# First feed-forward of a packed-attention kernel: block by block over both halves, output products of 512 tokens, a ninth tile for the rest

## The chip, the cores and the metric

The kernel runs on one core of one Trainium2 chip, as one launch with no arithmetic on the host. The metric is device time in microseconds (us) of that core, the median of several runs. The engines are PE (TensorE, matmuls; PEld is its weight load), DVE (VectorE), ACT (ScalarE), POOL (GpSimd) and SP (SyncE, which issues the DMAs).

## The reference, cut to what matters

```python
# q, k, v: (8, 8, 576, 64); p: (8, 8, 32, 64): 8 batches, 8 heads, 576 tokens, 32 packed rows
p_packed = softmax(scale * p @ k.T) @ v
out      = softmax(scale * q @ p_packed.T) @ p_packed
x = out.transpose(0, 2, 1, 3).reshape(4608, 512)
# first feed-forward, d_ff 1536
xn = x / sqrt(mean(x * x) + 1e-6) * rms_g
x1 = (silu(xn @ w_gate) * (xn @ w_val)) @ w_out
# second feed-forward, d_ff 2048
h = x1 @ w_in
return (h * cos(h)) @ w2_out
```

All weights come as 64-bit floats and are narrowed on the chip to 32 bits with integer operations; every large product is made of three matmuls over a high and a low part of both operands (`mm3`, L152 to L155).

## The kernel before, in words

**First stage.** The packed rows are computed for all batches and heads (L599 to L652). Beside it, weights are narrowed: `narrow_a` is an ACT operation and, for some weights, one of POOL; `narrow_b` is three or four operations of DVE (L139 to L148). A weight's `narrow_b` is put off to `w_late` (L640), which is called at the end of the round or, for the last rounds, at the top of the next (L625); those of the last two weights come at L625 of round 17. The attention of batch 0 (`bg0`) runs beside it from round 5; its last four steps come after the stage (L758).

**First feed-forward.** The loop at L811 has one round for each of 8 x 2 x 12 blocks: a batch `b`, a half `hf` of 288 tokens, a block `f` of 128 of the 1536 columns. In batches 1 to 7 the order is half 0 with all 12 blocks, then half 1. In batch 0 it is four blocks of half 0, the same four of half 1, and so on (`SEG`, L795), since its weights are still being narrowed. A round does this:
- `gv_block` (L696): 12 matmuls of 288 columns for gate and value, into two of the four PSUM tiles of the tag `mm`; then a sigmoid on ACT (L710) and two products on DVE (L711, L712), which read and so release those two tiles.
- `split_s` (L715): high part on ACT (L103), low part on DVE (L104), each of 288 tokens.
- `acc_block` for the block of two rounds before (`LAG`): 12 matmuls of 288 columns (four parts of 128 outputs, three each) into four PSUM tiles. When a half is complete (in batch 0: when four blocks of a half are), the sums are copied to `x1` by DVE (L743) and ACT (L744); in batch 0 the second and third groups of four are added to the first by DVE (L737). The result goes to DRAM (L746).
- `att_step`, twice in a round: steps of the attention of the batch after, a generator (`attend`, L215). It is given out evenly over the 48 slots of a batch (`N_ATT`, L802; in batch 0 from slot 10). Its PSUM tiles are `mm` too. Counts 13 and 14 are the two exponentials (L249), which need another ACT table than the sigmoid.
- at the rounds in `units`: `unit` (L540), which multiplies packed rows by narrowed weights (16 matmuls, `mps`, two `mm` tiles) and splits the result for a batch to come (ACT L103 and DVE L104, `wmhl`), followed by `wy_fetch`, the load of weights for the unit after the next.
- in batch 0, `b0_step` (L534): one weight of `B0_W` a round, `narrow_b` of the one before, the split of the one before that.
- from round 28, at seven rounds of a batch (`W2_AT`), one of the 32 tiles of the weights of the second feed-forward: load, `narrow` in one piece, store (L675 to L691).

**Second feed-forward.** Nine chunks of 512 tokens, 16 blocks each: `h_block` (12 matmuls of 512 columns), cosine on ACT and DVE (L888 to L894), product and split (`h_rest`), and `o_block`, three blocks later (`LAG_B`; 12 matmuls of 512 columns). The first chunk and the first weights are loaded and split in the last batch of the first feed-forward (L830 to L845, L857 to L861).

**Order.** Each engine works its instructions in the order of the program text as far as `order` reaches (L597 to block 6 of the second feed-forward, `OWN`); after that the framework's scheduler orders them. All DMAs are issued by SP, in order.

## Time and profile before

| | |
|---|---|
| runs | 1751.84, 1753.54, 1756.1 us; median 1753.54 us |
| profiled execution | 1755.67 us, of which its span is 1753.9 us |
| PE busy | 1676.0 us, 96% of the span |
| DVE busy | 1121.2 us, 64% |
| ACT busy | 835.9 us, 48% |
| POOL busy | 67.6 us, 4% |
| mean granted PE clock | 0.979 |

Matmuls overlap in the pipeline, so one of them is shown longer than the time by which it delays the next; what a stream of matmuls costs is the distance from one start to the next. PEclk is the granted clock as a share of 2.4 GHz; its lower level is 1.2 GHz. An idle time in brackets stands before the instruction, with what ended it. A wait is put down to the one that ended last.

### The profile page before, as it was taken

How to read it: one execution, taken by the hardware profiler on the slowest of the kernel's cores; microseconds unless marked ns; L12 is line 12 of the kernel's file. 1: busy time of each engine (PE TensorE's matmuls, PEld its weight loads, DVE VectorE, ACT ScalarE, POOL GpSimd, SP SyncE). 2: the span in 40 equal slices, each digit the busy share in tenths (PEclk: the TensorE clock that was granted, in tenths of full speed). 3: DMA queues.
4: the chain of work that ended last, by engine and by line, in shares of the span. 5: the costliest groups of instructions: out<-in, count | busy, mean ns of one | idle time of the engine just before them, and what ended most of it. 6: DMA issues, size and time to landing. Idle time of an engine off the chain costs nothing.

```text
span 1753.9 us, 28300 instructions
## 1 busy us (share of the span) xinstructions
PE 1676.0 (96%) x11184; PEld 1454.7 (83%) x11184; DVE 1121.2 (64%) x2184; ACT 835.9 (48%) x1599; POOL 67.6 (4%) x77
## 2 busy tenths in 40 slices
PE   7776879999999999999999999999999999999998
PEld 5555768999999999999999788888888888888887
DVE  2576887767767676766565765556565656555554
ACT  3454454444444444444445654555454545454443
POOL 0000331000000000000002000000000000000000
PEclk8887999999999999999999999999999999999999
DMA  9996543345353525332234200000000000000010
GB/s 205 254 270 187 145 128 121 130 147 173 133 179 102 193 96 185 129 119 76 87 104 154 73 24 25 24 25 24 25 24 25 24 25 24 25 1 25 0 25 24
DMA packets 88260, 164.89 MB, mean 94 GB/s; under 512 B 24128, under 2 KB 46656, under 8 KB 88128
## 3 DMA queue, kind: packets, MB, share of 16 engines
q1 hardware_dynamic: 88128, 163.09, 30.6%
q8 instruction: 88, 1.44, 0.3%
q14 instruction: 44, 0.36, 0.1%
HBM read 127.93 MB, written 35.13 MB: 93 GB/s over the span
## 4 chain that ended last, share of the span: by engine, by line
PE 81%; DVE 7%; DMA 6%; issue 4%; ACT 2%; SPq 1%; POOL 0%; DVEq 0%; ACTq 0%; POOLq 0%
PE ops L155 7%; PE ops L153 7%; PE ops L154 7%; PE hp L155 7%; PE hp L154 7%; PE hp L153 7%; PE gv L153 5%; PE acc L153 5%; DMA kn<-in_k_dram 5%; PE acc L154 5%; PE acc L155 5%; PE gv L154 5%; PE gv L155 5%; PE mps L548 3%; PE sp L233 1%
## 5 line engine op out<-in xcount | busy, mean ns | idle before, releaser
L153 PE MATMUL gv<-apt,wmhl 128*128 128x288 f32 x768 | 238.4, 310 | 12.1 <-DVE silu L711 9.3
L153 PE MATMUL acc<-shl,wohl 128*128 128x288 f32 x768 | 234.6, 305 | 1.0 <-ACT sq L293 1.0
L154 PE MATMUL acc<-shl,wohl 128*128 128x288 f32 x768 | 228.6, 298 | 0.0
L155 PE MATMUL acc<-shl,wohl 128*128 128x288 f32 x768 | 228.5, 297 | 0.0
L154 PE MATMUL gv<-apt,wmhl 128*128 128x288 f32 x768 | 228.0, 297 | 0.0
L155 PE MATMUL gv<-apt,wmhl 128*128 128x288 f32 x768 | 227.3, 296 | 0.0
L153 PE MATMUL ops<-w2hl,ghl 128*128 128x512 f32 x576 | 224.8, 390 | 1.7 <-ACT ghl L103 1.7
L154 PE MATMUL ops<-w2hl,ghl 128*128 128x512 f32 x576 | 224.8, 390 | 0.0
L154 PE MATMUL hp<-xhl,wmhl 128*128 128x512 f32 x576 | 224.1, 389 | 0.0
L155 PE MATMUL hp<-xhl,wmhl 128*128 128x512 f32 x576 | 224.1, 389 | 0.0
L153 PE MATMUL hp<-xhl,wmhl 128*128 128x512 f32 x576 | 224.1, 389 | 0.0
L155 PE MATMUL ops<-w2hl,ghl 128*128 128x512 f32 x576 | 223.2, 391 | 0.0
L901 DVE TENSOR_TENSOR r<-r,hp 128x512 f32<-128x512 f32 x144 | 98.9, 687 | 179.1 <-ACT r L894 179.0
L893 ACT ACTIVATE r<-r 128x512 f32<-128x512 f32 x144 | 91.1, 632 | 247.9 <-DVE r L892 247.9
L103 ACT ACTIVATE shl<-silu 128x288 fp32r<-128x288 f32 x192 | 85.3, 444 | 240.4 <-DVE silu L712 238.4
L153 PEld LDWEIGHTS gv<-apt,wmhl 128*128 128x128 f32 x768 | 145.3, 189 | 53.4 <-DVE silu L711 13.2
L888 ACT ACTIVATE kk<-hp,magic 128x512 f32<-128x512 f32 x144 | 99.1, 689 | 121.9 <-PE hp L155 121.9
L153 PEld LDWEIGHTS acc<-shl,wohl 128*128 128x128 f32 x768 | 145.6, 190 | 1.2 <-ACT sq L293 1.2
L154 PEld LDWEIGHTS gv<-apt,wmhl 128*128 128x128 f32 x768 | 145.9, 190 | 0.0
L154 PEld LDWEIGHTS acc<-shl,wohl 128*128 128x128 f32 x768 | 145.6, 190 | 0.0
L155 PEld LDWEIGHTS gv<-apt,wmhl 128*128 128x128 f32 x768 | 145.5, 189 | 0.0
L155 PEld LDWEIGHTS acc<-shl,wohl 128*128 128x128 f32 x768 | 145.1, 189 | 0.0
(128 smaller groups left out, 2952.4 us busy)
## 6 DMA issues: line engine op xcount, KB each, us to landing
wy<-wy SPq DMA_DIRECT2D x96, 512.0 KB, 4.1
kn<-in_k_dram SPq DMA_DIRECT2D x16, 576.0 KB, 7.8
vn<-in_v_dram SPq DMA_DIRECT2D x48, 192.0 KB, 6.9
qnat<-in_q_dram SPq DMA_DIRECT2D x32, 288.0 KB, 4.7
x_dram<-x SPq DMA_DIRECT2D x32, 288.0 KB, 2.6
x1raw<-x_dram SPq DMA_DIRECT2D x18, 512.0 KB, 3.8
raw<-in_moe_w_in_dram SPq DMA_DIRECT2D x16, 512.0 KB, 6.0
raw<-in_moe_w_out_dram SPq DMA_DIRECT2D x16, 512.0 KB, 5.2
```

The lines of the kernel that those rows point to most:

```text
L103: nc.scalar.activation(out=hi, in_=src, func=AF.Copy)
L153: nc.tensor.matmul(ps, lhi, rhi, start=first, stop=False)
L154: nc.tensor.matmul(ps, lhi, rlo, start=False, stop=False)
L155: nc.tensor.matmul(ps, llo, rhi, start=False, stop=last)
L233: nc.tensor.matmul(sp[:, i, 2 * c:2 * c + 2, :], qT[:, i, c * CP:(c + 1) * CP], bq[:, 2 * j + i], start=True, stop=True,)
L548: nc.tensor.matmul(ps[kt][h * NP:(h + 1) * NP], ppT[b // 4][rows, 4 * kt + h, n:n + NP], w_y[2 * u + kt][rows, j], start=True, stop=True,)
L888: nc.scalar.activation(out=kk, in_=hp, func=AF.Identity, scale=1.0 / TWO_PI, bias=magic[:, 0:1])
L893: nc.scalar.activation(out=r, in_=r, func=AF.Abs)
L901: nc.vector.tensor_tensor(out=r, in0=r, in1=hp, op=ALU.mult)
```

## The change

The first feed-forward goes block by block, each block over both halves, in every batch. The output product of a block is made of 512 tokens at once (`acc_block(n, f, d2)`: six matmuls of 512 columns a round, for two of the four parts), three rounds behind. The last 64 tokens of each batch are stored, block by block, in `s_dram`; when all batches are through, a ninth tile of 512 tokens is made of them, twelve blocks one after the other. The chunks of the second feed-forward are then the first 512 tokens of each batch and the ninth tile. The low part of a split moves to the start of the next round (`split_lo`). Narrowing is given out operation by operation. The two last `narrow_b` of the first stage move behind the attention of batch 0. The attention has one more empty count behind each of the two reductions, 45 counts in place of 43. The rounds of units, weights and loads move; the sine table is loaded in the ninth tile; two lags grow by one.

```diff
...
-    SEG = 4
+    REST = S - 512
+    R_LOAD, R_SPLIT, S_AT = (1, 2), (4, 5), (20, 21, 24 + 1, 24 + 2)
...
-    U_AT = {3: (0, 3), 9: (0, 4), 14: (0, 5), 18: (1, 0), 21: (1, 1), 24: (1, 2), 26: (1, 3), 28: (1, 4), 30: (1, 5)}
-    U_J = (16, 18, 20, 22, 25, 28)
+    U_AT = {3: (0, 3), 8: (0, 4), 14: (0, 5), 16: (1, 0), 18: (1, 1), 20: (1, 2), 22: (1, 3), 26: (1, 4), 30: (1, 5)}
...
-    B0_W = (15, -4, 16, -5, 17, -6, 18, 19, -7, 20, 21, 22, 23, -8, -9, -10, -11)
+    B0_W = (15, 16, 17, 18, 19, -4, 20, 21, -5, 22, 23, -6, 0, -7, 0, -8, 0, -9, 0, -10, 0, -11)
     B0_L, B0_LEAD = {15: (0,), 16: (1, 2), 17: (3,)}, 4
-    W_LOAD, W_SPLIT = (12, 13, 17, 18, 21, 22), (16, 17, 20, 21)
-    W2_I0, W2_AT, W2_POOL = 28, (1, 3, 5, 7, 11, 14, 18), False
-    T_END, F3_B, OWN = 2, 3, 6
-    LAG, LAG_B = 2, 3
+    W_LOAD, W_SPLIT = (4, 6, 14, 16), (9, 11, 17, 19)
+    W2_I0, W2_POOL = 28, False
+    T_END, F3_B, OWN = 2, 3, 16
+    LAG, LAG_B = 3, 4
...
-    ATT_FROM, ATT_TO, ATT_FROM0, N_ATT = 0, 48, 10, 43
-    BX, BS, BW = 0, 3, 6
+    ATT_FROM, ATT_TO, ATT_FROM0, N_ATT = 0, 48, 10, 45
+    BX, BS, BW = 10, 13, 12
...
+    s_dram = [dram.tile([128, 2, B * REST], F32, name=f"s_{f}") for f in range(NF1)]
...
-    def narrow_b(raw, y, pool):
+    def narrow_b(raw, y, pool, x=None):
...
-        if not pool:
-            nc.vector.tensor_scalar(out=y, in0=y, scalar1=TINY_HI, scalar2=None, op0=ALU.max)
...
+        if x in (None, 0) and not pool:
+            nc.vector.tensor_scalar(out=y, in0=y, scalar1=TINY_HI, scalar2=None, op0=ALU.max)
+        if x in (None, 1):
+            nc.vector.tensor_scalar(
...
+        if x in (None, 3):
+            nc.vector.scalar_tensor_tensor(
+                out=yi, in0=low, scalar=29, in1=yi, op0=ALU.logical_shift_right, op1=ALU.bitwise_or
+            )
...
             nc.vector.tensor_scalar(out=sm[:, 0], in0=sm[:, 0], scalar1=1e-9, scalar2=None, op0=ALU.add)
             nc.vector.reciprocal(out=sm[:, 1], in_=sm[:, 0])
             yield
+            if b:
+                yield
             nc.vector.tensor_tensor(
                 out=sf, in0=sf, in1=sm[:, 1].unsqueeze(2).to_broadcast([CP, n_s, NP]), op=ALU.mult
             )
...
     def b0_step(i):
-        b0_prep(i - 1, 1)
         b0_prep(i - 2, 2)
         b0_prep(i, 0)
         b0_load(i + B0_LEAD)
...
@@ -622,7 +632,8 @@
             u_kt(i + 1, [0, 1])
         if 1 < i:
             u_fin(i - 2)
-        w_late()
+        if i <= NG:
+            w_late()
         if i < NG:
             u_e(i)
...
+        w_last = w_late
+
         def w_late(ns=tuple(w_q), os=tuple(wo_q)):
...
     store(0)
-    w_late()
     assert not w_q and not wo_q and att_done[0] == ATT_U
...
-    a3 = fst.enter_context(tc.tile_pool(name="a3", bufs=3, reuse_waits="tile"))
-    f1 = fst.enter_context(tc.tile_pool(name="f1", bufs=1, reuse_waits="tile"))
+    a3 = fst.enter_context(tc.tile_pool(name="a3", bufs=4, reuse_waits="tile"))
     f2 = fst.enter_context(tc.tile_pool(name="f2", bufs=2, reuse_waits="tile"))
     f3 = fst.enter_context(tc.tile_pool(name="f3", bufs=F3_B, reuse_waits="tile"))
     xst = ExitStack()
-    x1p = xst.enter_context(tc.tile_pool(name="x1p", bufs=1, reuse_waits="tile"))
+    f1 = xst.enter_context(tc.tile_pool(name="f1", bufs=1, reuse_waits="tile"))
...
-    def w2_narrow(keep):
-        if len(w2_raw) > keep:
-            (kind, f, a), raw = w2_raw.pop(0)
-            y = late["w2"].tile(list(raw.shape[:3]), F32, tag="ny", name="ny")
-            narrow(raw, y, W2_POOL)
+    def w2_narrows():
+        w2_fetch()
+        yield
+        w2_fetch()
+        it, raw = w2_raw.pop(0)
+        nxt = None
+        while True:
+            kind, f, a = it
+            if nxt is None:
+                y = late["w2"].tile(list(raw.shape[:3]), F32, tag="ny", name="ny")
+                narrow_a(raw, y, W2_POOL)
+                yield
+            else:
+                y, nxt = nxt, None
+            for x in range(4):
+                narrow_b(raw, y, W2_POOL, x)
+                if x < 3:
+                    yield
             dst = w2i_dram[f][:, 2 * a:2 * a + 2, :] if kind == "i" else w2o_dram[f]
             w2_done.add((kind, f, a))
             nc.sync.dma_start(out=dst, in_=y if kind == "i" else y[:, 0])
+            if not w2_raw:
+                return
+            it, raw = w2_raw.pop(0)
+            nxt = late["w2"].tile(list(raw.shape[:3]), F32, tag="ny", name="ny")
+            narrow_a(raw, nxt, W2_POOL)
+            w2_fetch()
+            yield
...
     def split_s(b, hf, f, t):
-        sh = s_t[b, hf, f] = f3.tile([128, 2, HALF], F32R, tag="shl", name="shl")
-        hilo(t, sh[:, 0], sh[:, 1])
-
-    def acc_block(b, hf, f):
-        n = NF1 if b else SEG
-        if f % n == 0:
-            acc_t[b, hf] = [ps_acc.tile([128, HALF], F32, tag="acc", name="acc") for _ in range(KD)]
-        sh = s_t.pop((b, hf, f))
+        if hf == 0:
+            s_t[b, f] = f3.tile([128, 2, S], F32R, tag="shl", name="shl")
+        sh, cols = s_t[b, f], slice(hf * HALF, (hf + 1) * HALF)
+        nc.scalar.activation(out=sh[:, 0, cols], in_=t, func=AF.Copy)
+        return b, f, hf, t, sh, cols
+
+    def split_lo(b, f, hf, t, sh, cols):
...
+        if hf:
+            stores.append((s_dram[f][:, :, b * REST:(b + 1) * REST], sh[:, :, TOK:].bitcast(F32)))
...
+    part = None
...
+    def load_s(f):
+        sh = s_t[B, f] = a3p[0].tile([128, 2, TOK], F32R, tag="apt", name="shl")
+        nc.sync.dma_start(out=sh.bitcast(F32), in_=s_dram[f])
+
+    def acc_block(n, f, d2):
+        if f == 0:
+            pool, tag = (psb[0], "mm") if n == B else (ps_acc, "acc")
+            acc_t[n, d2] = [pool.tile([128, TOK], F32, tag=tag, name="acc") for _ in range(2)]
+        sh = s_t[n, f]
         wo = wo_t[f]
-        for d in range(KD):
+        for r in range(2):
+            d = 2 * d2 + r
             mm3(
-                acc_t[b, hf][d], wo[:, 0, d * 128:(d + 1) * 128], wo[:, 1, d * 128:(d + 1) * 128],
-                sh[:, 0], sh[:, 1], f % n == 0, f % n == n - 1,
+                acc_t[n, d2][r], wo[:, 0, d * 128:(d + 1) * 128], wo[:, 1, d * 128:(d + 1) * 128],
+                sh[:, 0, :TOK], sh[:, 1, :TOK], f == 0, f == NF1 - 1,
             )
...
-                if f >= n:
-                    x1 = x1_t[hf, d2]
-                    for r in range(2):
-                        nc.vector.tensor_tensor(out=x1[:, r], in0=acc_t[b, hf][2 * d2 + r], in1=x1[:, r], op=ALU.add)
-                else:
-                    if b:
-                        x1 = late["x"].tile([128, 2, HALF], F32, tag="x1", name="x1")
-                    else:
...
-                    nc.vector.tensor_copy(x1[:, 0], acc_t[b, hf][2 * d2])
-                    nc.scalar.activation(out=x1[:, 1], in_=acc_t[b, hf][2 * d2 + 1], func=AF.Copy)
-                if f == NF1 - 1:
-                    nc.sync.dma_start(out=x1_at, in_=x1)
...
+        if d2:
+            s_t.pop((n, f))
+        if f == NF1 - 1:
+            x1 = raw_p.tile([128, 2, TOK], F32, tag="raw", name="x1")
+            nc.vector.tensor_copy(x1[:, 0], acc_t[n, d2][0])
+            nc.scalar.activation(out=x1[:, 1], in_=acc_t[n, d2][1], func=AF.Copy)
+            nc.sync.dma_start(out=x1_dram[:, 2 * d2:2 * d2 + 2, n * TOK:(n + 1) * TOK], in_=x1)
...
-        late["x"] = fst.enter_context(tc.tile_pool(name="x1s", bufs=3, reuse_waits="tile"))
...
     for _ in bg0:
         pass
+    w_last()
+    w_late()
     att_load(1)
...
-    seq = [(0, hf, x * SEG + f) for x in range(NF1 // SEG) for hf in range(2) for f in range(SEG)]
-    seq += [(b, hf, f) for b in range(1, B) for hf in range(2) for f in range(NF1)]
+    seq = [(b, f, hf) for b in range(B) for f in range(NF1) for hf in range(2)]
...
     for i in range(len(seq) + LAG):
-        b, hf, f = seq[min(i, len(seq) - 1)]
-        j = i % B1
+        b, f, hf = seq[min(i, len(seq) - 1)]
+        j = i - b * B1
...
+            if part:
+                split_lo(*part)
             t = gv_block(b, hf, f)
+            b0_prep(i - 1, 1, 0)
+            b0_prep(i - 1, 1, 1)
             att_step(2 * i)
-            split_s(b, hf, f, t)
+            b0_prep(i - 1, 1, 2)
+            part = split_s(b, hf, f, t)
+        elif part:
+            part = split_lo(*part)
         if i >= LAG:
             acc_block(*seq[i - LAG])
-            att_step(2 * i + 1)
-            b, hf, f = seq[i - LAG]
-            if (b, hf) == (B - 1, 0):
-                if f == BX:
-                    load_x(0)
-                if f in (BS, BS + 2):
-                    split_x(0, (f - BS) // 2)
-                if f >= BW and f < BW + 4:
-                    w2_split(f - BW + NF1)
-                if f >= BW - 2 and f < BW + 2:
-                    w2_load(f - BW + 2 + NF1)
-                if f >= NF1 - 2:
-                    w2_load(f - NF1 + 2)
-            if (b, hf) == (B - 1, 1):
-                w2_split(f)
-                if f + 2 < NF1:
-                    w2_load(f + 2)
-            b, hf, f = seq[min(i, len(seq) - 1)]
+            if i < len(seq):
+                att_step(2 * i + 1)
+        b0_prep(i - 1, 1, 3)
         store(0)
         if i in units:
...
-        if i < len(seq) and b == B - 1:
+        if b == B - 1:
             if j in W_LOAD:
                 wm_load(wm_next.pop(0))
             if j in W_SPLIT:
                 wm_split()
-        if i >= W2_I0 and j in W2_AT:
-            w2_fetch()
-            w2_narrow(len(w2_items) > 0)
+            if j == BX:
+                load_x(0)
+            if j in (BS, BS + 2):
+                split_x(0, (j - BS) // 2)
+            if BW <= j < BW + 4:
+                w2_load(j - BW + NF1)
+            if BW + 2 <= j < BW + 6:
+                w2_split(j - BW - 2 + NF1)
+            if j in S_AT:
+                load_s(S_AT.index(j))
+            if B1 <= j < B1 + 2:
+                w2_load(j - B1)
+        if i >= W2_I0:
+            if i == W2_I0:
+                w2_bg = w2_narrows()
+            next(w2_bg, None)
+    assert not w2_items and not w2_raw
+    warm = f2.tile([128, 1], F32, tag="silu", name="warm")
+    for f in range(NF1):
+        for d2 in range(2):
+            acc_block(B, f, d2)
+        if f + len(S_AT) < NF1:
+            load_s(f + len(S_AT))
+        w2_split(f)
+        if f == NF1 // 2:
+            nc.scalar.activation(out=warm, in_=halfpi, func=AF.Sin)
+        if f + 2 < NF1:
+            w2_load(f + 2)
+        if f in R_LOAD:
+            wm_load(wm_next.pop(0))
+        if f in R_SPLIT:
+            wm_split()
     assert not wm_next
...
+    ps_h = ctx.enter_context(tc.tile_pool(name="ps_h", reuse_waits="tile", bufs=4, space=PSUM))
     ps_o = ctx.enter_context(tc.tile_pool(name="ps_o", reuse_waits="tile", bufs=4, space=PSUM))
-    ps_h = ctx.enter_context(tc.tile_pool(name="ps_h", reuse_waits="tile", bufs=4, space=PSUM))
...
-        r0 = n * TOK + t * 128
         off = 0
         while off < 128:
-            b, u = divmod(r0 + off, S)
+            if n < B:
+                b, u = n, t * 128 + off
+            else:
+                b, u = divmod(t * 128 + off, REST)
+                u += TOK
...
-            if n == 0 and f in (3, 5, 9, 11):
-                wm_split(wm_p if f < 6 else b4, nc.vector)
-            if n == 0 and f in (3, 5):
-                wm_load(("w", NCK + f // 4))
+            if n == 0 and f in (4, 6):
+                wm_split(b4, nc.vector)
+            if n == 0 and f in (0, 1):
+                wm_load(("w", NCK + f))
...
```

## Rows read from the trace of the kernel before

**Rows 1.** Windows: busy time by engine, granted clock, DMA share; five stretches, two left out.

```profile
core 0: us, PE busy (x) PEld busy (x) DVE busy (x) ACT busy (x) POOL busy (x), PEclk, DMA share, GB/s
168.62:300.00 131.38, 113.34 (x854) 102.81 (x855) 104.07 (x205) 58.14 (x126) 38.05 (x26) 0.94 0.42 129
...
369.46:467.44 97.98, 97.34 (x813) 91.06 (x819) 71.86 (x155) 44.58 (x100) 1.76 (x2) 1.00 0.43 148
962.00:1050.00 88.00, 86.35 (x373) 70.71 (x372) 59.29 (x97) 50.55 (x80) 0.00 (x0) 0.98 0.17 55
```

**Rows 2.** Waits of PE, 300 to 960 us: total, times, longest (us).

```profile
PE gv L153 <- DVE silu L711: 3.5, 5, 0.9
```

**Rows 3.** Chain that ended last, 168 to 300 us, shares by line (cut by the view).

```profile
by line: PE gv L153 6.3%; issue 6.1%; DVE silu L712 5.6%; DVE wy L145 5.5%; DVE ny L145 5.1%; PE gv L155 5.0%; PE gv L154 5.0%; DVE wy L148 4.4%; DVE silu L711 4.3%; PE acc L153 3.8%; PE acc L154 3.7%; DVE wy L142 3.7%; PE acc L155 3.7%; DV
```

**Rows 4.** Waits of DVE, 168 to 300 us: total, times, longest (us).

```profile
DVE shl L104 <- ACT shl L103: 8.6, 15, 1.5
DVE silu L711 <- ACT silu L710: 8.1, 7, 3.0
```

**Rows 5.** Timeline of PE: first and last of 36 matmuls of 288 columns.

```profile
175.58 0.30 PE L153 MATMUL acc<-shl,wohl 128*128 128x288 f32 x1
...
180.25 0.29 PE L155 MATMUL acc<-shl,wohl 128*128 128x288 f32 x1
```

**Rows 6.** Timeline of PE: first and last of 55 matmuls of 512 columns.

```profile
1199.65 0.39 PE L155 MATMUL ops<-w2hl,ghl 128*128 128x512 f32 x1
...
1211.89 0.39 PE L155 MATMUL ops<-w2hl,ghl 128*128 128x512 f32 x1
```

**Rows 7.** Timeline of DVE: the first of eight narrowing operations, and what follows them.

```profile
163.62 0.41 DVE L139 TENSOR_SCALAR wy<-wy 128x512 f32<-128x512 f32 x1
...
168.12 1.54 DVE L104 TENSOR_TENSOR apt<-atp,apt 128x288 fp32r<-128x288 f32 x4
```

**Rows 8.** Groups of instructions by line and shape, DVE.

```profile
L737 DVE TENSOR_TENSOR x<-acc,x 128x288 f32<-128x288 f32 x16 | 6.2, 445 | 0.0
...
L743 DVE COPY x<-acc 128x288 f32<-128x288 f32 x32 | 13.0, 449 | 0.0
...
L104 DVE TENSOR_TENSOR wmhl<-mps,wmhl 128x512 fp32r<-128x512 f32 x96 | 61.9, 686 | 44.3 <-ACT wmhl L103 44.2
```

**Rows 9.** Timeline of PE: first gate matmul, a wait in batch 0, second feed-forward.

```profile
168.62 0.61 PE L153 MATMUL gv<-apt,wmhl 128*128 128x288 f32 x1 [2.68 <-DVE apt L104]
...
236.95 0.74 PE L265 MATMUL atp<-ident,s 96*128 96x96 f32 x3 [5.78 <-DVE s L257]
...
974.12 0.50 PE L153 MATMUL ops<-w2hl,ghl 128*128 128x512 f32 x1 [1.65 <-ACT ghl L103]
...
978.83 0.39 PE L153 MATMUL hp<-xhl,wmhl 128*128 128x512 f32 x1
```

**Rows 10.** Timeline of ACT: table loads, in batch 0, batch 1, second feed-forward.

```profile
222.97 1.28 ACT L249 ACT_TABLE_LOAD   x1
...
231.83 1.28 ACT L710 ACT_TABLE_LOAD   x1
...
325.40 1.28 ACT L249 ACT_TABLE_LOAD   x1
...
329.17 1.28 ACT L710 ACT_TABLE_LOAD   x1
...
967.63 1.28 ACT L894 ACT_TABLE_LOAD   x1
```

**Rows 11.** Windows, as rows 1: the stretch of batch 0 with two exponentials.

```profile
225.00:240.00 15.00, 7.58 (x46) 7.10 (x46) 10.00 (x20) 9.43 (x15) 5.70 (x4) 0.82 0.12 37
```

**Rows 12.** Waits of SP, 300 to 960 us: total, times, longest (us).

```profile
SPq L491 <- PE mps L548: 165.5, 35, 10.7
```

**Rows 13.** DMA issues: count, KB each, median us from issue to landing.

```profile
wy<-wy SPq DMA_DIRECT2D x96, 512.0 KB, 4.1
...
c<-cd SPq DMA_DIRECT2D x16, 32.0 KB, 5.8
```

More of the change, by code (lines that the diff above doesn't have):

```diff
@@ L118, in load_w, with narrow @@
         return t
-    def narrow(raw, y, pool=True, part=None):
+    def narrow(raw, y, pool=True, part=None, x=None):
         if part != 1:
@@ L478, in w_prep, with wy_prep @@
         wy_prep(n, part)
-    def wy_prep(n, part):
+    wy_done = set()
+    def wy_prep(n, part, x=None):
         t, j = divmod(n, 2)
@@ L483, in wy_prep @@
             w_y[t] = wm_p.tile([128, 2, 512], F32, tag="wy", name="wy", bufs=4)
-        narrow(w_raw[n], w_y[t][:, j:j + 1], n >= W_KV, part)
-        if j and part:
+        narrow(w_raw[n], w_y[t][:, j:j + 1], n >= W_KV, part, x)
+        if part and x in (None, 3):
+            wy_done.add(n)
+        if j and part and x in (None, 3):
             stores.append((wy_dram[t], w_y[t]))
@@ L518, in b0_load, with b0_prep @@
     def b0_load(x):
-        if x < len(B0_W):
+        if x < len(B0_W) and B0_W[x]:
             n = B0_W[x]
             (wy_load if n >= 0 else wo_load)(abs(n))
-    def b0_prep(x, part):
-        if 0 <= x < len(B0_W):
-            n = B0_W[x]
+    def b0_prep(at, part, x=None):
+        if 0 <= at < len(B0_W) and B0_W[at]:
+            n = B0_W[at]
             if part == 2:
@@ L669 @@
     psb[0] = ps_gv = fst.enter_context(tc.tile_pool(name="ps_gv", reuse_waits="tile", bufs=4, space=PSUM))
-    w2_items = [("i", f, a) for f in range(NF2 // 2) for a in range(2)] + [("o", f, 0) for f in range(NF2)]
+    w2_items = [("i", f, a) for f in range(NF2 // 2) for a in range(2)] + [("o", (f + NF1) % NF2, 0) for f in range(NF2)]
     w2_raw = []
@@ L861 @@
                 wm_split()
-        if i >= W2_I0 and j in W2_AT:
-            w2_fetch()
-            w2_narrow(len(w2_items) > 0)
+            if j == BX:
[30 more added lines that the diff above has]
+            wm_split()
     assert not wm_next
-    assert not w2_items and not w2_raw
     fst.close()
```

34 lines of the change are left out of this document (14 added, 20 removed).

## The prediction, made before the changed kernel was run

> **What bounds the kernel now.** I read the windows first, by stage, since the change lies in one of them. In a middle batch of the first feed-forward PE is busy 97.3 of 98.0 us and DVE 71.9 [rows 1]: PE's stream of matmuls is the bound, and from 300 to 960 us PE waits 3.5 us in all [rows 2]. Batch 0 is another matter: from 168.62 to 300 PE is busy 113.3 of 131.4 us, so 18.0 idle, and the granted clock is 0.94 [rows 1]; as it has two levels, 12% of the stretch, 15.8 us, lay at 1.2 GHz, which cost at most half of that, 7.9 us. DVE is busy 104.1 us there, and the chain that ended last runs through its narrowing operations (5.5, 5.1, 4.4 and 3.7%) and the two products (5.6 and 4.3%) about as much as through PE [rows 3]: DVE, worked in order, bounds batch 0. At the start of the second feed-forward PE waits once, and its clock falls to 0.98 on average [rows 1].
>
> **Product of 512 tokens.** What a matmul costs is the distance of starts. At 288 columns it is 4.67 us / 35 = 0.1334 us [rows 5]; at 512 it is 12.24 / 54 = 0.2267 us [rows 6]. So a matmul pays 0.0133 us besides its columns. Before, 8 x 2 x 12 blocks x 12 = 2304 matmuls: 307.4 us. After, 8 x 12 x 12 + 144 in the ninth tile = 1296: 293.8 us. The columns are the same, 1008 matmuls are gone: **-13.6 us**, all on the path, since PE is the bound. The ninth tile's 144 x 0.2267 = 32.6 us are in that sum; nothing covers them, but each batch is shorter by 24 x 0.24 = 5.8 us, and comes to 92.2 us. The Trainium skill, "TensorE: Matmul & The Clock Gate", section "Wait — 56ns, not 53.3ns?", speaks against this gain: it puts the fixed cost of a matmul at about 2.5 ns, by which the term would be an estimated 1008 x 2.5 ns = 2.5 us. The trace does not agree with that rule: its 13.3 ns is five times as much.
>
> **Before the first matmul.** The four low parts of `apt` stood behind eight narrowing operations on DVE from 163.62 to 168.12 us [rows 7], and PE waited 2.68 us for them [rows 9]. They move behind. **-2.5 us** (0.2 for what is then late: DVE's low part behind ACT's high part). The 4.5 us of DVE are not saved but come in batch 0.
>
> **Batch 0.** DVE's 104.1 us lose 16 additions (7.1 us [rows 8]) and four copies (1.8 us [rows 8]; the two new ones come behind the stretch), and get the moved 4.5 us and one unit more by round 24, two operations of 0.686 us [rows 8]: 101.1 us. Its idle 27.3 us hold 8.6 in which the low part waited for the high one, and 8.1 for the sigmoid [rows 4]. The first go, since the low part now comes a round later, behind work that it would have waited for anyway. Of the second I take half away: four table loads fall between 222.97 and 231.83 [rows 10], since a sigmoid stands between the two exponentials; with 45 counts on 38 slots both fall in block 10. That leaves 14.7 us idle and a stretch of 115.8 us. PE's own need is 131.4 - 18.0 - 7.9 - 23 blocks x 0.24 = 100 us, so DVE stays the bound. The gain is 15.6 us, of which 5.5 are in the first term: **-10.1 us**. The ends: nothing, if the idle time is what DVE's chain needs; and 24.8 us, 14.7 more than taken, if DVE has no idle time at all (101.1 us, which is just over PE's own 100).
>
> **Tables in batches 1 to 6.** The new counts cost something here. Slot x hands out 43(x+1)/48 counts before and 45(x+1)/48 after. Counts 13 and 14, the exponentials, fell on slots 14 and 15, both in block 7 and behind its sigmoid; the trace shows the one pair of loads, at 325.40 and 329.17 [rows 10]. Now they fall on slots 13 and 14: block 6, and block 7 behind the sigmoid. So a batch has two pairs, 2.57 us more of ACT, 15.4 us in six batches, and ACT also has a unit in the same round (j = 6). What PE loses is between nothing, as now with one pair [rows 2], and what it lost in the one place with two: 225 to 240, where PE is busy 7.58 of 15 us [rows 11], 7.4 us each or 44 us. I take 0.8 each, **+5 us**, near the lower end, since DVE is not full here (71.9 of 98), and a round's PSUM tiles are needed again only two rounds later.
>
> **Start of the second feed-forward.** PE waited 1.65 us for the first `ghl`, then did twelve matmuls at the lower clock level in 974.12 to 978.83, 4.71 us for 2.72 [rows 9]. On the way of that `ghl` stood a table load of 1.28 us [rows 10]. The load moves into the ninth tile, and `LAG_B` of four gives a further block of 12 x 0.2267 = 2.72 us before `ghl` is needed: **-3.6 us**; the ends are -1.3, the table alone, and -3.7. The swap of the PSUM pools lets the first block begin without waiting for the ninth tile's copies.
>
> **Costed at nothing.** Steps of narrowing in batches 1 to 6: the DVE's free quarter covers them, six tiles a batch for seven; were it full, the most is the 3.5 us waited now. The moved units, splits and loads: behind them PE has its stream; POOL does the same splits, two of them in the ninth tile. `load_x(0)` at round 10 of the last batch needs buffers that POOL's splits of rounds 9 and 11 release, so SP stands there a round or two, with a store of `s` queued behind. SP gets 96 stores of 64 KB and 12 loads of 512 KB, and has 14 fewer of `x1`. A store has three rounds, 11.5 us, until ACT writes its buffer again; landing takes 5.8 us at the worst of the rows that come near, and SP's fetch waits 165.5 / 35 = 4.7 us on average [rows 12, 13], together 10.5. The longest wait, 10.7, would not be covered and stop ACT and then PE by some 5 us, once: the end of the range. In the ninth tile a load has three blocks, 8.2 us, against 4.1 us [rows 13]. `split_lo` now heads DVE's queue in a round: the products, and by them two PSUM tiles, wait behind it when ACT is late, which is the case of the tables above. `OWN` and the chunk order leave PE's full stretch as it is.
>
> **Sum.** -13.6 - 2.5 - 10.1 + 5 - 3.6 = -24.8 us, against the profiled execution's 1755.67 us (span 1753.9, 1.8 around it): 1730.9. That execution lay 2.1 us above the median of the runs, 1753.54, so I predict **1729 us**.
>
> **Rivals.**
> - Batch 0 keeps its idle time: DVE's chain there is a matter of work, not of order, and the moved 4.5 us fill what is freed. For it: DVE is the chain [rows 3]. Against: 8.6 us of waits are plainly gone [rows 4]. 1729 + 10 = 1739.
> - Batch 0 packs: every wait of DVE goes, PE is fed, its clock stays up. 1729 - 15 = 1714. For it: PE waits there in few large pieces, as the 5.78 us before `atp` [rows 9], which go with the second table pair. Against: of the 14.7 us of idle time of DVE that would have to go, the rows name only four.
> - Columns alone: a matmul of 288 columns costs 288/512 of 0.2267 us when it stands among 512-wide ones, and the first term vanishes: 1729 + 14 = 1743. Against: 36 matmuls in a row of gate, value and output products keep 0.1334 us [rows 5]. The rule of the Trainium skill that is cited above ("TensorE: Matmul & The Clock Gate") comes near to this case.
> - Slower, by the tables: in batches 1 to 6 the sigmoid between the exponentials comes so late that both PSUM pairs are held and PE stands, as at 225 to 240 [rows 11]. At 7.4 us each 1729 - 5 + 44 = 1768. It decides from (24.8 + 5) / 6 = 5 us a batch. Against: at 225 to 240 DVE was also full of narrowing.
>
> **How the numbers follow.** About 0.2%, 3.5 us, is what a measurement of this kernel can tell from no change. Forecast 0.63 (its own range 1720 to 1738), idle kept 0.15, packed 0.13, columns alone 0.03, tables 0.06. The first four lie more than 3.5 us below the median: 0.94. Of that, 0.02 goes to a kept batch 0 together with dear tables, which would end level: faster 0.92, same 0.02, slower 0.06. The range 1712 to 1745 takes in the packed and the kept batch 0 and the columns, and leaves out the tables at their full price and what lies below 1712.
>
> **What would show it.** In the changed kernel: output products 0.227 us apart; a middle batch of some 93 us with about 1 us of PE idle; 168 to the end of batch 0 some 16 us shorter with DVE near 88% busy; in batches 1 to 6 two pairs of table loads, with PE waits for L711 behind them; PE without a pause into the ninth tile and for its 33 us, and no wait at the first `ops`. The prediction is wrong if the fixed cost of 0.0133 us does not hold beside 512-wide matmuls, if PE waits over 2 us a batch behind the tables, or if SP's queue holds a store back.

## The result, and the profile after

The changed kernel takes 1730.43 us (median of 1725.12, 1735.22, 1734.43 and 1726.43), the kernel before 1752.69 us beside it: ratio 0.9871, 95% interval 0.983 to 0.9912. Forecast were 1729 us and a range of 1712 to 1745, with 92% for faster. The changed kernel is 1.3% faster. The sign, the size and the mechanism of the largest term hold; two terms of the sum were mis-sized and partly cancel; that the median came within 1.4 us of the forecast is in part luck.

The profiled execution took 1725.12 us, with a span of 1723.3. That is 30.6 us below that of before, while the medians differ by 22.3. Of these, 10.4 lie ahead of the last transposes (`atp`) of the first stage, which start at 163.76 us before and 153.33 here behind the same instructions: the loads move 206 GB/s in the first 40 us before and 250 here. A repeat of the same changed kernel had 222, and its transposes started at 159.33. So I compare stages, not whole executions: each is cut by starts in PE's timeline, at a batch's first gate matmul, the first `hp` and the end.

| us | before | after | difference | forecast |
|---|---|---|---|---|
| last `atp` to first gate matmul | 4.86 | 1.89 | -3.0 | -2.5 |
| batch 0 | 121.18 | 109.47 | -11.7 | -6.6 products, -10.1 |
| batch 1 | 100.21 | 93.75 | -6.5 | -5.8 products, +0.8 |
| batches 2 to 6, mean | 97.80 | 92.66 | -5.1 | -5.8 products, +0.8 |
| batch 7, ninth tile | 82.41 | 113.41 | +31.0 | +27.8, products alone |
| second feed-forward | 792.50 | 788.16 | -4.3 | -3.6 |

The products are laid on these cuts by counting (the forecast's own stretch, which ran to 300 us and so 10.2 us into batch 1, had 5.5 us of them in batch 0): batch 0 holds 22 rounds of output products before (12 x 0.1334 us each) and 21 after (6 x 0.2267), the last cut 26 and 27 and the ninth tile.

First the windows of the changed kernel by stage, columns as in [rows 1]: batch 0, a middle batch, batch 7 with the three rounds that trail, the ninth tile, the start of the second feed-forward.

```profile
core 0: us, PE busy (x) PEld busy (x) DVE busy (x) ACT busy (x) POOL busy (x), PEclk, DMA share, GB/s
155.22:264.69 109.47, 97.17 (x661) 78.83 (x659) 92.49 (x186) 53.73 (x117) 38.42 (x25) 0.97 0.53 168
358.44:451.10 92.66, 92.12 (x661) 78.69 (x660) 66.49 (x150) 46.62 (x99) 2.80 (x2) 1.00 0.50 154
821.73:901.64 79.91, 78.27 (x484) 68.66 (x482) 43.25 (x87) 31.70 (x70) 10.60 (x8) 1.00 0.32 94
901.64:935.14 33.50, 32.93 (x145) 26.95 (x144) 9.89 (x14) 11.61 (x19) 5.07 (x4) 1.00 0.83 306
935.14:1024.00 88.86, 88.86 (x394) 73.57 (x392) 57.21 (x92) 47.36 (x75) 0.00 (x0) 1.00 0.20 60
```

The middle batch is PE from end to end, 0.5 us idle, as before [rows 1], only shorter. The ninth tile is 33.5 us for 144 matmuls, and 24 of them lie between these two rows of PE's timeline in the changed kernel, 5.44 / 24 = 0.2267 us each, as forecast:

```profile
901.64 0.39 PE L157 MATMUL acc<-shl,wohl 128*128 128x512 f32 x1
...
907.08 0.39 PE L157 MATMUL acc<-shl,wohl 128*128 128x512 f32 x1
```

The second feed-forward starts without a pause at the full clock, where it had 0.98. Batch 0 still leaves PE idle for 12.3 us, at a granted clock of 0.97 in place of 0.94. DVE is busy 84% of it, not the forecast 88%.

Next the waits of PE in the changed kernel (total, times, longest, in us) in batches 1 to 6, which answers to [rows 2].

```profile
PE gv L157 <- DVE silu L742: 2.2, 6, 0.4
PE atp L271 <- DVE silu L742: 2.1, 6, 1.2
```

ACT's timeline in the changed kernel, the table loads of a middle batch, and the sine's in the ninth tile: two pairs a batch, as counted beforehand, where [rows 10] shows one.

```profile
479.06 1.28 ACT L253 ACT_TABLE_LOAD   x1
...
482.18 1.28 ACT L741 ACT_TABLE_LOAD   x1
...
483.90 1.28 ACT L253 ACT_TABLE_LOAD   x1
...
486.40 1.28 ACT L741 ACT_TABLE_LOAD   x1
...
924.34 1.28 ACT L913 ACT_TABLE_LOAD   x1
```

Now DVE's waits in batch 0 of the changed kernel, 155.22 to 264.69. In [rows 4], which reach to 300 us, the high part and the sigmoid stand with 8.6 and 8.1 us; on batch 0 alone they were 7.6 and 6.6, and are 0.5 and 4.9 now. New are 5.0 us (4.5 and 0.5) for POOL: a narrowing's second DVE operation waits for POOL's, which stands behind a split of some 1.4 us.

```profile
DVE silu L742 <- ACT silu L741: 4.9, 6, 2.5
DVE ny L144 <- POOL ny L134: 4.5, 4, 1.3
DVE ssq L300 <- ACT sq L299: 1.3, 2, 0.7
DVE s L317 <- POOL ri L311: 1.0, 1, 1.0
...
DVE shl L754 <- ACT shl L750: 0.5, 1, 0.5
DVE wy L144 <- POOL wy L134: 0.5, 1, 0.5
```

And PE's timeline in the changed kernel at the places that answer to [rows 9], with two waits that the forecast has not: the output product now waits for the low part.

```profile
153.33 2.18 PE L271 MATMUL atp<-ident,s 96*128 96x96 f32 x12 [2.12 <-DVE ppT L457]
155.22 0.59 PE L157 MATMUL gv<-apt,wmhl 128*128 128x288 f32 x1
...
212.49 0.50 PE L158 MATMUL acc<-shl,wohl 128*128 128x512 f32 x1 [2.20 <-DVE shl L754]
...
884.36 0.50 PE L158 MATMUL acc<-shl,wohl 128*128 128x512 f32 x1 [1.64 <-DVE shl L754]
...
910.53 0.50 PE L157 MATMUL acc<-shl,wohl 128*128 128x512 f32 x1 [0.57 <-DMA shl<-s]
...
948.75 0.39 PE L157 MATMUL ops<-w2hl,ghl 128*128 128x512 f32 x1
```

The low part of 212.49 stood on DVE behind a softmax reduction and two narrowing steps, as the timeline of DVE in the changed kernel shows:

```profile
208.94 0.94 DVE L257 TENSOR_REDUCE sm<-s 96x24 f32<-96x768 f32 x1
...
210.71 0.62 DVE L148 SCALAR_TENSOR_TENSOR wy<-wo,wy 128x512 int32<-128x512 int32 x1
211.37 0.69 DVE L152 SCALAR_TENSOR_TENSOR wy<-wo,wy 128x512 int32<-128x512 int32 x1
211.98 0.45 DVE L754 TENSOR_TENSOR shl<-silu,shl 128x288 fp32r<-128x288 f32 x1
```

### The profile page after: what moved, and what is told of

Same layout as the page of the kernel before. It is cut to its first block, busy times and chain, and to the rows that moved or that the text cites. A ratio compares the mean times of both kernels' runs of the same rounds, so it can differ in the third digit from the quotient of the medians.

```text
span 1723.3 us, 26510 instructions
## 1 busy us (share of the span) xinstructions
PE 1660.1 (96%) x10176; PEld 1377.2 (80%) x10176; DVE 1092.7 (63%) x2150; ACT 847.8 (49%) x1596; POOL 80.2 (5%) x81
## 4 chain that ended last, share of the span: by engine, by line
PE 76%; DVE 4%; ACT 3%; issue 1%; DMA 1%; SPq 0%; POOL 0%; DVEq 0%; ACTq 0%
PE hp L158 8%; PE ops L157 8%; PE ops L158 8%; PE hp L157 8%; PE ops L159 8%; PE hp L159 8%; PE gv L157 5%; PE acc L157 4%; PE acc L159 4%; PE acc L158 4%; PE gv L158 4%; PE gv L159 4%; PE mps L558 2%; PE sp L237 1%; ACT L741 1%
## 5 line engine op out<-in xcount | busy, mean ns | idle before, releaser
L157 PEld LDWEIGHTS gv<-apt,wmhl 128*128 128x128 f32 x768 | 145.2, 189 | 51.9 <-DVE silu L742 10.2
L157 PE MATMUL acc<-shl,wohl 128*128 128x512 f32 x432 | 176.0, 407 | 0.6 <-DMA shl<-s 0.6
L158 PE MATMUL acc<-shl,wohl 128*128 128x512 f32 x432 | 170.2, 394 | 5.2 <-DVE shl L754 5.2
L159 PE MATMUL acc<-shl,wohl 128*128 128x512 f32 x432 | 170.6, 395 | 0.0
L943 DVE TENSOR_SCALAR kk<-kk 128x512 f32<-128x512 f32 x144 | 61.4, 426 | 116.4 <-ACT kk L942 116.4
L157 PEld LDWEIGHTS hp<-xhl,wmhl 128*128 128x128 f32 x576 | 108.2, 188 | 22.5
L159 PEld LDWEIGHTS hp<-xhl,wmhl 128*128 128x128 f32 x576 | 108.1, 188 | 22.6
```

The costliest lines, as they stand in the source:

```text
L157: nc.tensor.matmul(ps, lhi, rhi, start=first, stop=False)
L158: nc.tensor.matmul(ps, lhi, rlo, start=False, stop=False)
L159: nc.tensor.matmul(ps, llo, rhi, start=False, stop=last)
L943: nc.vector.tensor_scalar(out=kk, in0=kk, scalar1=-MAGIC, scalar2=None, op0=ALU.add)
```

## The experiments

All are edits of the changed kernel, but for the first. The cuts are those of the table above; "first feed-forward" is the first gate matmul to the first `hp`, 779.92 us in the changed kernel. Single times hold the first stage's spread of some 10 us, so the cuts decide.

**The kernel before, again.**

> The kernel before once more. The profiled executions differ by 30.6 us, and 10.4 of them lie ahead of the transposes after the first stage, where the same instructions run (163.76 against 153.33 us). Theory: that is a difference between executions, in the rate of the DMAs of the first stage (206 against 250 GB/s in the first 40 us); then the first gate matmul of this run starts somewhere between 158 and 169 us, and not always at 168.6. Rival: the change shortens the first stage by 10 us; then it starts within 1 us of 168.6 here and within 1 us of 155.2 in all runs made from the changed kernel. From the first gate matmul to the first matmul of the second feed-forward both expect 792 to 794 us.

Measured: 121.23, 100.21, 97.84, 82.41 and 792.31 us in the order of the table, all within 0.2 of the first profile. The first gate matmul starts at 166.22 us here, and between 155.97 and 163.78 in the runs made from the changed kernel, so the rival falls. An estimate from spans agrees: the eleven executions of the kernel before that were timed beside the repeat of the changed kernel have spans of 1743.6 to 1751.4 us; less the 1590.2 us from `atp` to the end in the table, 153.4 to 161.2 are left for the first stage, and the runs made from the changed kernel have 153.0 to 161.9.

The cuts are good to some tenths of a us, but not all of them equally: in runs whose edit doesn't touch them, batch 0 came out between 109.4 and 110.4 us, batch 1 between 92.7 and 93.8, and the last cut between 112.9 and 113.7.

**Halves of 256 columns in the second feed-forward.**

```diff
+        for c in (0, 256):
             for d in range(KD):
-                mm3(hp, ..., x[:, 0, d], x[:, 1, d], ...)
+                mm3(hp[:, c:c + 256], ..., x[:, 0, d, c:c + 256], x[:, 1, d, c:c + 256], ...)
```

> The changed kernel with every first product of the second feed-forward made of two matmuls of 256 columns in place of one of 512: 1728 matmuls more, the same columns. Theory: a matmul pays 0.0133 us besides its columns, so the second feed-forward is longer by 1728 x 0.0133 = 23.0 us. Rival: columns alone, 0 us. By the 2.5 ns that the Trainium skill's page on TensorE gives for a matmul, an estimate of 4.3 us.

Measured: 814.09 us for the second feed-forward, 25.9 more, or 0.0150 us for each of the 1728 added matmuls. In PE's timeline of this run, 24 matmuls of 256 columns lie between these two rows, 2.87 / 24 = 0.1196 us each:

```profile
1200.18 0.28 PE L157 MATMUL hp<-xhl,wmhl 128*128 128x256 f32 x1
...
1203.05 0.40 PE L157 MATMUL ops<-w2hl,ghl 128*128 128x512 f32 x1
```

Two of them less one of 512 is 0.0125 us, 21.6 in 1728; the other 4.3 lie in the twelve matmuls of 512 between, 2.75 us in place of 2.72, 144 times. So a matmul pays a fixed part beside wide ones too, and "columns alone" falls. The fixed 2.5 ns that the Trainium skill gives ("TensorE: Matmul & The Clock Gate", section "Wait — 56ns, not 53.3ns?") would have made this run 1728 x 2.5 ns, an estimated 4.3 us longer; the measurement does not agree.

**One pair of table loads.** 44 counts, begun one slot earlier in batch 0.

```diff
-    ATT_FROM, ATT_TO, ATT_FROM0, N_ATT = 0, 48, 10, 45
+    ATT_FROM, ATT_TO, ATT_FROM0, N_ATT = 0, 48, 9, 44
```

> The changed kernel with 44 counts in place of 45, and in batch 0 from slot 9: both exponentials fall behind the same sigmoid in all batches, and the sigmoid's table is loaded 8 times in place of 14. Theory: the second pair of loads costs PE about 0.5 us in each of batches 1 to 6, so a middle batch goes from 92.66 to about 92.2 us, and the first feed-forward is shorter by about 3 us. Rival 1: the second pair costs PE nothing; 92.6 to 92.7 us. Rival 2: the pair hides more, 0.8 us or over, as predicted; 91.9 or less.

Measured: one pair of loads a batch, 2.8 us less of ACT, and a middle batch of 93.78 us, 1.1 longer. PE's waits in five of them (all batches from 364 to 833 us):

```profile
PE atp L271 <- DVE silu L742: 5.7, 5, 1.1
PE gv L157 <- DVE silu L742: 1.8, 5, 0.4
```

That is none of the three that were expected. The second pair costs nothing that its removal gives back: the transposes now meet a product that is late. As every later step of the attention shifts with the count, the price of a pair by itself stays open. The prediction's rival "slower, by the tables" falls, since the middle batches became shorter with two pairs.

**Low part at once.**

```diff
 def split_s(b, hf, f, t):
     ...
     nc.scalar.activation(out=sh[:, 0, cols], in_=t, func=AF.Copy)
+    nc.vector.tensor_tensor(out=sh[:, 1, cols], in0=t, in1=sh[:, 0, cols].bitcast(F32), op=ALU.subtract)
...
 def split_lo(b, f, hf, t, sh, cols):
-    nc.vector.tensor_tensor(out=sh[:, 1, cols], in0=t, in1=sh[:, 0, cols].bitcast(F32), op=ALU.subtract)
```

> The changed kernel with the low part of a split made in the same round, directly behind the high part, as before the change. Theory: DVE waits again some 0.5 us a round for ACT where it is not held up already; in batch 0, where DVE bounds, that makes 109.5 us about 5 us longer (8.6 us of such waits stood there before); in the middle batches DVE has room, 92.66 stays within 0.3. Rival: the delayed low part gains nothing, since DVE waits elsewhere instead; batch 0 within 1.5 us of 109.5.

Measured: batch 0 109.05 us (109.47), a middle batch 94.19 (92.66). Undoing the delay costs nothing in batch 0, where I had counted on it. But it doesn't bring the waits of before back there either, since steps of narrowing now stand on DVE ahead of the low part, while ACT makes the high one; DVE's waits in batch 0 of this run have

```profile
DVE shl L751 <- ACT shl L750: 1.0, 2, 0.5
```

In the last cut the delay costs something: 111.51 us here in place of 113.41, as the wait for the low part at 884 us is not there. In each middle batch, where I had not counted on it, it is worth 1.5 us: PE's waits for the products there, five batches from 366 to 837 us, are

```profile
PE atp L271 <- DVE silu L742: 5.5, 5, 1.1
PE gv L157 <- DVE silu L742: 4.8, 5, 1.0
```

**Narrowing of batch 0 in one piece**, at the round's end as before.

```diff
 def b0_step(i):
+    b0_prep(i - 1, 1)
...
-            b0_prep(i - 1, 1, 0)
-            b0_prep(i - 1, 1, 1)
             att_step(2 * i)
-            b0_prep(i - 1, 1, 2)
...
-        b0_prep(i - 1, 1, 3)
```

> The changed kernel with the narrowing of batch 0 in one piece at the end of a round again (three or four DVE operations in a row), all else as changed. Theory: batch 0 is bound by the amount of DVE's work (92.5 us in 109.5), not by its order, as the run with the low part in the same round showed (109.05); then batch 0 stays within 1.5 us of 109.5. Rival: the small steps are what keeps PE fed; batch 0 is 4 us longer or more. From batch 1 on nothing changes: 92.66 within 0.1.

Measured: batch 0 111.69 us, 2.2 longer, between the two that were expected; the rest as it was (93.43, 92.69, 113.31). PE waits 6.4 us for the first product in place of 4.5. DVE's waits for the high part of `shl` stay at 0.5; new are 5.0 us for that of the units (`wmhl`).

**Narrowing of the second feed-forward's weights in one piece**, every fourth round, at the place of the last step.

```diff
-            for x in range(4):
-                narrow_b(raw, y, W2_POOL, x)
-                if x < 3:
-                    yield
+            for x in range(3):
+                yield
+            narrow_b(raw, y, W2_POOL)
```

> The changed kernel with the narrowing of the second feed-forward's weights in one piece in every fourth round (2.25 us of DVE in a row), at the same rate. Theory: where DVE has a quarter of its time free the burst still holds the gate product back behind it, and the next attention transposes or gate matmuls wait for their PSUM tile; a middle batch goes from 92.66 to between 93.2 and 95. Rival, as the prediction had it: it costs nothing, 92.66 within 0.2. Batch 0 does not change: 109.5 within 1.5.

Measured: a middle batch of 98.52 us, 5.9 longer and beyond the 93.2 to 95 expected, with batch 0 as it was (109.46), and a first feed-forward of 814.12, 34.2 longer than in the changed kernel and 21.3 longer than before the change (792.78). PE's waits in five middle batches of this run:

```profile
PE atp L271 <- DVE silu L741: 9.4, 5, 1.9
PE gv L157 <- DVE silu L741: 6.8, 9, 1.3
```

That is 3.2 us a batch, 2.5 more than in the changed kernel, of the 5.9. A part of the rest is the clock. In the windows of a middle batch of this run, columns as above, PE stands for 1.9 us in the first, and in the four us of the second the granted clock is 0.66; the third is the stretch in which it is under 1.00:

```profile
511.06:515.06 4.00, 2.10 (x12) 1.58 (x11) 3.83 (x8) 1.04 (x3) 0.00 (x0) 0.91 0.39 98
515.06:519.06 4.00, 4.00 (x22) 3.70 (x21) 2.61 (x7) 1.23 (x3) 0.00 (x0) 0.66 0.37 117
509.80:521.88 12.08, 10.18 (x66) 8.10 (x64) 8.51 (x20) 3.50 (x9) 0.00 (x0) 0.86 0.28 77
```

A mean of 0.86 over 12.08 us is, as an estimate, 0.14 x 12.08 = 1.7 us of the full clock lost in a batch; the other 1.7 of the 5.9 I did not trace. DVE is full where PE stands, 3.83 of 4 us, though it is busy only 70% of the batch (68.86 of 98.88 us). Under the new order the small steps, which I had costed at nothing, decide the sign of the whole change.

**The two last narrowings in front of batch 0's attention**, as before.

```diff
+    w_last()
+    w_late()
     for _ in bg0:
         pass
-    w_last()
-    w_late()
```

> The changed kernel with the two last narrowings of the first stage ahead of the attention's last transposes again. Theory: the first gate matmul comes 2.5 to 3.5 us later behind the transposes (4.9 us after the first transpose in place of 1.5 to 1.9), and batch 0, which no longer begins with 4.5 us of narrowing on DVE, is shorter by 2 to 4 us, so that the sum of both stays within 1 us. Rival, as the prediction had it: the start costs 2.5 us more and batch 0 gives little of it back (under 1 us).

Measured, in PE's timeline of this run: the last `atp`, the first gate matmul, that of batch 1.

```profile
156.30 2.18 PE L271 MATMUL atp<-ident,s 96*128 96x96 f32 x12 [1.98 <-DVE ppT L457]
161.17 0.61 PE L157 MATMUL gv<-apt,wmhl 128*128 128x288 f32 x1 [2.69 <-DVE apt L106]
...
267.79 0.29 PE L157 MATMUL gv<-apt,wmhl 128*128 128x288 f32 x1
```

The wait of 2.69 us is back, and batch 0 is 106.62, 2.85 shorter. From `atp` to batch 1 it is 111.49 us here, and 264.69 - 153.33 = 111.36 in the changed kernel: the move is worth nothing. What it gains ahead of the first matmul is lost in the first four rounds, which are 2.85 us longer in the changed kernel.

**DVE in place of POOL for the splits in the last batch.**

```diff
             if j in W_SPLIT:
-                wm_split()
+                wm_split(eng=nc.vector)
```

> The changed kernel with the low parts of the second feed-forward's weights made by DVE in place of POOL in the last batch. In the changed kernel's trace PE stands 1.64 us at 884 us for a low part that took 1.51 us in place of 0.45 while POOL subtracted. Theory: POOL's work slows DVE's operation; with DVE alone the wait goes, and the stretch from batch 7 to the second feed-forward falls from 113.41 to between 111.3 and 112.3 us. Rival: the wait is DVE's place behind the weights' high part on ACT, and stays: within 0.5 us of 113.4, or longer, as DVE has 5.5 us more to do.

Measured: 112.53 us for the last cut, 0.9 less, which lies between the two that were expected, and the wait for the low part 0.6 us in place of 1.64. The timelines of the changed kernel have the low part ahead of 884.36 at three times its length, while POOL subtracts:

```profile
881.02 2.97 POOL L106 TENSOR_TENSOR wmhl<-wmraw,wmhl 128x512 fp32r<-128x512 f32 x2 [17.99 <-ACT wmhl L105]
...
882.79 1.51 DVE L754 TENSOR_TENSOR shl<-silu,shl 128x288 fp32r<-128x288 f32 x1
```

and in this run, where POOL rests, at 0.45:

```profile
890.23 0.45 DVE L754 TENSOR_TENSOR shl<-silu,shl 128x288 fp32r<-128x288 f32 x1
```

The Trainium skill, "SBUF — State Buffer", section "SBUF: two separate sides", says that DVE and GpSimd share a port pair as an exclusive lock: a DVE operation with two SBUF inputs is held for the whole of a POOL instruction that reads SBUF and started first. The trace agrees, as far as spans on POOL, which are rough, can show it: the low part has two such inputs and ends at 884.30, just behind POOL's 883.99.

**POOL's operation in front of the split.**

```diff
 def b0_step(i):
-    b0_prep(i - 2, 2)
     b0_prep(i, 0)
+    b0_prep(i - 2, 2)
```

> The first operation of a narrowing stands on POOL directly in front of the split of another weight instead of behind it; nothing else changes. In the changed kernel DVE waits five times for that POOL operation in batch 0, 5.0 us in all (4.5 and 0.5), each time behind a POOL split of 1.4 to 1.6 us. Theory one, this new wait is what batch 0 is short of its forecast: the waits for POOL fall under 1 us and batch 0, first gate matmul to first gate matmul of batch 1, falls from 109.5 us to about 106 (3.4 us less, the miss). Theory two, DVE's chain in batch 0 is set by its work and by the sigmoid, and time gained at these places is waited at the next sigmoid: batch 0 stays within 1 us of 109.5 and the waits for L741 grow by what those for POOL lose. The middle batches stay at 92.7 in both.

Measured: no wait for POOL's `ny` or `wy` is left, and batch 0 takes 107.88 us, 1.6 less. Neither theory has it whole: a third of the removed 5.0 us comes back. The sigmoid waits in batch 0 stay at 4.9, so they did not take the rest. It went into DVE's operations: DVE is busy 95.79 us in batch 0 in place of 92.49, with 186 operations in both, as the window of this run has it:

```profile
156.54:264.42 107.88, 97.03 (x660) 80.14 (x659) 95.79 (x186) 53.94 (x117) 37.78 (x25) 0.95 0.54 170
```

The operation that had waited now runs beside POOL's split, as the timelines of this run show:

```profile
222.24 1.28 POOL L524 TENSOR_TENSOR wohl<-ny,wohl 128x512 fp32r<-128x512 f32 x1
...
222.43 1.38 DVE L144 TENSOR_SCALAR ny<-ny 128x512 int32<-128x512 int32 x1
```

In the changed kernel's timeline it had waited, and then took 0.43 us:

```profile
222.65 0.43 DVE L144 TENSOR_SCALAR ny<-ny 128x512 int32<-128x512 int32 x1 [1.06 <-POOL ny L134]
```

The 19 operations of this line in batch 0 take 13.50 us here and 8.05 in the changed kernel; other operations are some 2.1 shorter. So the time goes while POOL works, in whichever order its two operations stand.

**A lag of three.**

```diff
-    LAG, LAG_B = 3, 4
+    LAG, LAG_B = 3, 3
```

> LAG_B back to three in the changed kernel; the sine table stays in the ninth tile. In the changed kernel ghl's high part ends 11.37 us and its low part 12.1 us after the first hp; with three blocks between, the first ops could start at 48 x 0.2267 = 10.9 us. Theory of the prediction, table and lag each do a part: PE waits 0.5 us for the high part and about 0.3 for the low one, and the second feed-forward from the first hp is longer than the 788.16 us of the changed kernel by 0.8 us, and by up to 2.0 more if the clock drops behind the wait. Rival, the table alone does it and the fourth lag is worth nothing: no wait at the first ops, 788.2 us.

Measured: the second feed-forward takes 789.52 us, 1.4 more. PE's timeline has a first `ops` 11.42 us behind the first `hp` (48 x 0.2267 = 10.9 without a wait):

```profile
953.30 0.50 PE L157 MATMUL ops<-w2hl,ghl 128*128 128x512 f32 x1 [0.38 <-ACT ghl L105]
...
956.44 0.39 PE L157 MATMUL hp<-xhl,wmhl 128*128 128x512 f32 x1
```

The wait makes 0.5 of the 1.4 us. The twelve matmuls between the two rows take 3.14 in place of 2.72, 0.4 more, and the last twelve of the kernel, from 1721.46 us, lose another 0.4 in the same way; the kernel before, also with a lag of three, loses it there too. The granted clock is 1.00 throughout. So of the -4.3 us the fourth lag gives 1.4, and the table with what else is new there 2.9 (792.4 less 789.5).

**The changed kernel again, and three edits together** (narrowings first, POOL's operation first, splits on DVE), timed beside the kernel before on one chip.

> The changed kernel as it is, beside the version below and the kernel before on the same chip: a ratio of about 0.987 to the kernel before, as in the result, and the cuts of the result (batch 0 109.5 us, middle batches 92.7, last batch with ninth tile 113.4) where nothing of them depends on the execution.

> Three edits together: the two last narrowings of the first stage stand before the last attention steps of batch 0 again, POOL's part of a narrowing stands in front of its split, and in the last batch DVE makes the low parts of the weight splits in place of POOL. If the gains of the single edits add up: batch 0 about 105 us (109.5 less 2.85 less 1.6) but first matmul 2.7 us later behind the narrowing, last batch with ninth tile 112.5 us, so that the first feed-forward takes about 774.5 us and the whole some 2.5 us less than the changed kernel. If DVE's chain takes back in batch 0 what it is given: first feed-forward 776 us or more and no difference to the changed kernel beyond 1 us.

Measured: the changed kernel 1727.45 us, ratio to the kernel before 0.9877 (0.9858 to 0.9895); the three edits 1722.89 us, ratio 0.9867 (0.9841 to 0.9892). The intervals overlap, so the times don't show the second to be faster than the first. In its profile the cuts are shorter: batch 0 105.01 us (109.45 in the repeat), the last cut 111.59 (113.35), the first feed-forward 773.03 (779.24). 3.0 us go back at its start, where `atp` to gate matmul is 4.86 again; 3.2 remain. In batch 0 the single gains add up, 109.47 - 2.85 - 1.59 = 105.03.

## Why the prediction was right, and where it was not

**Products: right.** -13.6 forecast; by counting, -13.5 on the cuts, and middle batches of 92.66 us for 92.2 to 93 forecast. The distance of 0.2267 us is there in the ninth tile, and the run with halves shows that a matmul's fixed part holds beside wide ones, 0.0125 us for 0.0133. The groups of the changed kernel show 432 matmuls on each of the three lines of `mm3`, 1296 in all, one of them here.

```profile
L158 PE MATMUL acc<-shl,wohl 128*128 128x512 f32 x432 | 170.2, 394 | 5.2 <-DVE shl L754 5.2
```

**Before the first matmul: right in place (-3.0 for -2.5), without worth.** The experiment shows all of it paid back in batch 0. I had put the 4.5 us into DVE's sum there, but then took the idle time that I let vanish to be independent of it.

**Batch 0: mis-sized.** -10.1 beyond the products was forecast, -11.7 + 6.6 = -5.1 came. The term that was mis-sized is DVE's idle time. The window and DVE's waits of the kernel before on batch 0 alone are

```profile
168.62:289.80 121.18, 103.14 (x765) 93.56 (x765) 98.46 (x192) 54.60 (x118) 38.05 (x26) 0.94 0.43 131
DVE shl L104 <- ACT shl L103: 7.6, 13, 1.5
DVE silu L711 <- ACT silu L710: 6.6, 6, 3.0
```

DVE's busy time fell by 6.0 us (98.46 to 92.49) where 3.0 were forecast, its idle time by 5.7 (22.7 to 17.0) where 12.6 were (27.3 to 14.7). The waits that the forecast let go did go, from 7.6 to 0.5 and from 6.6 to 4.9. The forecast had no waits in their place, and they came: 5.0 us for POOL, and 2.3 for `sq` and `ri` in the attention. On PE's side an output product stands 3.6 us for a low part that queues behind other work, 2.0 with the low part at once. The reason given for the first waits, "since the low part now comes a round later", is not shown: with the low part at once they are 1.0 us, with the narrowing in one piece 0.5, so either of the two edits alone keeps them away. What they were worth is open, as neither run brought them back. The small steps gave 2.2, more than the spread of this cut. The gain lies midway between the forecast and the rival "idle kept"; "packed" falls.

**Tables in batches 1 to 6: mis-sized the other way.** +5 forecast; the six batches lost 32.2 us, the products alone are 34.6, so +2.4. That the pairs would come I had right, and PE waits only 0.7 us a batch (2.2 and 2.1 in six); that they cost 0.8 each is not shown, since one pair less made the batch longer.

**Costed at nothing: wrong for two edits.** Narrowing in steps was bounded by 3.5 us, "the most" being what PE waited for before. Against the kernel before, the steps cost nothing, as forecast; but under the new order they are needed. In one piece the narrowing costs 34 us in the changed kernel, since a DVE that is free for a quarter of a batch is full for some microseconds, just when the transposes need a tile. The delayed low part is worth 1.5 us a middle batch, 9 in six, and costs 1.9 in the last cut. Whether the rounds and places of before would have done as well under the new order was not tried.

The last cut is 31.0 - 27.8 = 3.2 us over the count of its products. The late low part at 884 us makes 1.9 of them, as the run with the low part at once shows, and 0.9 of these go when POOL does not subtract beside it. In the ninth tile the load of the fourth block comes late: two starts, at 910.53 and 910.87, lie 0.96 and 0.34 us behind the ones before them in place of 0.23, 0.8 us in all. These loads take longer than the 4.1 us that the forecast took for them:

```profile
shl<-s SPq DMA_DIRECT2D x12, 512.0 KB, 6.2
```

The other 0.5 I did not trace. No store of `s` was seen to stop PE: ACT has no wait for one.

**Start of the second feed-forward: right**, -4.3 for -3.6; the end given was -3.7. Full clock, no wait at the first `ops`. Of what is over, 0.4 is the fourth lag's at the last output products, which the forecast did not have.

**Sum.** Batch 0 gave 5.0 us less, the last cut 3.2 and the products 0.1, the tables cost 2.6 less, the two starts gave 1.2 more: some 4.5 of the forecast 24.8 are missing. The stages come to -20.2, the medians to -22.3 and, in the repeat, -20.3. So the change is worth about 20 us; 1729 came so close to 1730.43 because misses partly cancel, and because some 2 us of the -22.3 are the first stage's, which the change leaves as it is.

## What to carry to other kernels

Where an engine works in order and is the bound, a wait removed from its trace is worth only what a run shows: here 5.0 us were worth 1.6, since the operations that had waited took longer instead. Look at an engine's busy time beside its waits, and see whether an undo brings the wait back before you price it: here it did not. An engine that is free on the average of a stage can still be full for the few microseconds in which the bounding engine needs it; cutting a block of 2 us into four steps was worth more under the new order than the change's main term. Compare stages by cuts at fixed instructions, when another stage varies by as much as the effect.

## What was not expected of the hardware

- The first stage's loads move 206 to 228 GB/s in the first 40 us in nine of the fourteen traces, and 239 to 262 in five; the changed kernel itself had 250 and 222. The last transposes of the stage start at 159.3 to 163.8 us in the nine and at 153.0 to 156.3 in the five. Both traces of the kernel before are among the nine. The cause is open.
- In two places a DVE operation beside a split on POOL shows no idle time ahead of it and takes some three times as long: 1.51 us for 0.45 with two inputs, 1.38 for 0.43 with one.
